# Attention with decay and a gated convolution layer: the last 64 tokens of two batches in one output chunk, three slots for gated products side by side, and another order of the work

## The chip, the cores and the metric

The kernel runs on one core of one Trainium2 chip. The metric is device time in microseconds (us) of one execution. Engines are named as the profile names them: PE is TensorE (PEld its weight loads), DVE VectorE, ACT ScalarE, POOL GpSimd, SP the engine that issues most DMAs (SPq its queue).

## What is computed

There are 8 batches of 8 heads, 576 tokens, 64 values per head. The first half is causal attention whose scores lose, from a key to a later query, the sum of the logs of a forget factor between them:

```python
scores = q @ k.T / sqrt(64) + (cum[query] - cum[key])   # cum = cumsum(log(f)), causal
attn   = softmax(scores);  x = attn @ v                  # x: [8, 576, 512], heads side by side
```

The second half is a layer on x with 512 inputs, 1024 inner channels and 512 outputs:

```python
h    = relu(x @ w_in)                                    # [8, 576, 1024]
conv = conv_w[0]*h[t-1] + conv_w[1]*h[t] + conv_w[2]*h[t+1]   # per channel, zero at both ends
out  = (h * sigmoid(conv)) @ w_out                       # [8, 576, 512], float32
```

## The kernel before

The program is a list of named tasks. Each task belongs to an engine, names the tasks it follows, and takes and gives slots of small pools (PSUM tiles `ps`, four of 128x1024; probability tiles, V tiles, inner tiles `ht` and `u`, gated products `hg`, output tiles `ob`). A long string, `ORDER` (line 18), gives the one order in which all tasks are issued, so it sets each engine's own order; `name@ENGINE` picks the engine where several can do a task. Each engine works through its tasks strictly in that order and waits where data or a slot is late.

The tasks, with their lines. A group `hb` of four heads is half a batch.

- `q`, `fi`, `rw`, `v`, `wi`, `wo` are loads on SP: transposing loads of q and k (L178), rows of the decay (L200, L201, L192, L194), V (L207), the weights (L496). `cl` (L170, L172, L184) clamps q and k rows on ACT or DVE; for the first two groups PE turns plain loads (`tp`, L164) and `cl` copies them out. `va` (L215, L217) casts V to 16 bits and `wic`, `woc` (L504) the weights, on POOL, ACT or DVE.
- `sd`, `so`, `st` are scores on PE (L310 and, for masks and the first heads' decay, L313 to L318); `ed`, `eo`, `et` their exponentials on ACT (L351, L368, L330); `md`, `mt` the causal masks of later groups on POOL (L354, L333).
- `pv` (L387, L392) is attention times V on PE, `n` (L400, L401) divides by the sum on DVE, `t` (L410) turns the result on PE and `tx` (L413) copies it to `xt`; the last two groups are turned by DMA (L416).
- For each batch `b` and each of 8 blocks of 128 inner channels: `f` (L425, PE) x times w_in, `r` (L435, ACT) relu, `c` and `d` (L440, L442, DVE) the two convolution steps, `a` (L445, ACT) tanh into `hg`, `g` (L449, DVE) the gated product in `hg`.
- `o` (L456, L460, PE) is the output: five chunks per batch, four of 128 tokens and one of the last 64; `e` (L466, L471) copies PSUM to `ob`, and `s` (L477, L482, L486) stores it.

In a chunk of 128 tokens the 8 gated blocks are 128x128 weights and 512 columns of w_out stream past them: 8 matmuls. In the chunk of 64 tokens (line 460) the weights are 64 columns wide; each block is used twice, with 256 columns of w_out each, the second into the other 64 partitions of PSUM: 16 matmuls, one copy of 128x256, two stores of 64x256. `hg` has two slots, one per batch in flight, given back when chunk 4 of the batch is done; the first plain loads of q and k also lie in them. In the last batch the output tasks are cut to one matmul each (`o7.c.ff`), so that they can start when one gated block is there, and each chunk has a copy and a store of its own.

Of the kernel before, what the change touches and what calls it, by code (L numbers as in the profile page):

```python
# [7 lines left out]
FP32 = mybir.dt.float32  # L8
FP16 = mybir.dt.float16
# [47 lines left out]
def kernel(  # L57
# [38 lines left out]
    dpool = ctx.enter_context(tc.tile_pool(name="dram", bufs=1, space=bass.MemoryType.DRAM))  # L96
# [49 lines left out]
    def ps_of(name):  # L146
        return ps_t[slot[name, "ps"]]


    def raw(hb):  # L150
        t = hg_t[slot[f"ld{hb}", "hg"]]
        return t.rearrange("p f s -> p (f s)").bitcast(FP32).rearrange("p (i x) -> p i x", i=4)
# [278 lines left out]
    def hg_of(b, ff):  # L431
        return hg_t[slot[f"h{b}", "hg"]][:, ff, :]
# [4 lines left out]
    def conv(b, ff, part):  # L437
        ht, u = ht_of(b, ff), u_t[slot[f"c{b}.{ff}", "u"]]
        if part == 0:
            nc.vector.scalar_tensor_tensor(u, ht[:, 0:S], cwt[:, ff, 0:1], ht[:, 1:1 + S], op0=ALU.mult, op1=ALU.add)  # L440
        else:
            nc.vector.scalar_tensor_tensor(u, ht[:, 2:2 + S], cwt[:, ff, 1:2], u, op0=ALU.mult, op1=ALU.add)  # L442

    def tanh(b, ff):
        nc.scalar.activation(hg_of(b, ff), u_t[slot[f"c{b}.{ff}", "u"]], AF.Tanh, scale=cw[:, ff, 1:2])  # L445

    def gate(b, ff):
        hv = hg_of(b, ff)
        nc.vector.scalar_tensor_tensor(hv, hv, 1.0, ht_of(b, ff)[:, 1:1 + S], op0=ALU.add, op1=ALU.mult)  # L449

    def ffn2(b, first, c, ffs):
        ps = ps_of(first)
        for ff in ffs:
            kw = dict(start=(ff == 0), stop=(ff == NFF - 1))
            if c < 4:
                nc.tensor.matmul(ps[:, 512 * (c % 2):512 * (c % 2 + 1)], hg_of(b, ff)[:, 128 * c:128 * (c + 1)],  # L456
                                 w_out_f16[:, ff, :], **kw)
            else:
                for a in range(2):
                    nc.tensor.matmul(ps[64 * a:64 * (a + 1), 0:256], hg_of(b, ff)[:, 512:576],  # L460
                                     w_out_f16[:, ff, 256 * a:256 * (a + 1)], skip_group_check=True, **kw)

    def evac(name, first, c, e):
        n = 1024 if c < 4 else 256
        ob = ob_t[slot[name, "ob"]].rearrange("p j c -> p (j c)")
        (nc.scalar.copy if e == "ACT" else nc.vector.tensor_copy)(ob[:, 0:n], ps_of(first)[:, 0:n])  # L466
# [206 lines left out]
```

## Time and profile before

| what | us |
|---|---|
| median of the three runs shown | 248.97 |
| these runs | 248.34, 248.97, 250.13 |
| span of the profiled execution, core 0 | 248.9 |
| PE, DVE, ACT, POOL busy in it | 232.9, 215.9, 211.1, 46.0 |
| mean granted TensorE clock | 0.998 |

The page gives the span as the profiled execution's time and no other time of that execution beside it. Busy time counts an instruction from its start to its end. Matmuls overlap, so their mean duration (379 ns for 512 columns) is more than the time from one to the next; the chain of waits, in which a group of eight takes 1.73 us, shows the latter. Times in windows and timelines are us from the span's start.

### The profile page before, as it was taken

How to read it: one execution, taken by the hardware profiler on the slowest of the kernel's cores; microseconds unless marked ns; L12 is line 12 of the kernel's file. 1: busy time of each engine (PE TensorE's matmuls, PEld its weight loads, DVE VectorE, ACT ScalarE, POOL GpSimd, SP SyncE). 2: the span in 40 equal slices, each digit the busy share in tenths (PEclk: the TensorE clock that was granted, in tenths of full speed). 3: DMA queues.
4: the chain of work that ended last, by engine and by line, in shares of the span. 5: the costliest groups of instructions: out<-in, count | busy, mean ns of one | idle time of the engine just before them, and what ended most of it. 6: DMA issues, size and time to landing. Idle time of an engine off the chain costs nothing.

```text
span 248.9 us, 6646 instructions
## 1 busy us (share of the span) xinstructions
PE 232.9 (94%) x2750; PEld 151.3 (61%) x2750; DVE 215.9 (87%) x328; ACT 211.1 (85%) x286; POOL 46.0 (18%) x76
## 2 busy tenths in 40 slices
PE   0899999879899999999999999999999999999993
PEld 0787785557556856666556765577557756645441
DVE  5654278999999999999999999997999999999961
ACT  2766958999999999979999899998999999767642
POOL 8000411101021501002203070045012502000000
PEclk9999999999999999999999999999999999999999
DMA  7987999999998999999999999899960590223345
GB/s 199 297 157 171 253 226 238 178 276 180 264 201 155 261 173 237 244 250 250 211 271 275 230 188 266 235 230 154 244 188 3 145 320 7 50 47 108 121 153 191
DMA packets 117062, 48.81 MB, mean 196 GB/s; under 512 B 106402, under 2 KB 107618, under 8 KB 117032
## 3 DMA queue, kind: packets, MB, share of 16 engines
q1 hardware_dynamic: 116578, 47.51, 85.3%
q0 software_dynamic: 208, 0.51, 0.7%
q8 instruction: 21, 0.34, 0.6%
q10 hardware_dynamic: 246, 0.37, 0.5%
q14 instruction: 9, 0.07, 0.1%
HBM read 21.11 MB, written 10.17 MB: 126 GB/s over the span
## 4 chain that ended last, share of the span: by engine, by line
PE 68%; DVE 12%; ACT 9%; DMA 6%; issue 3%; ACTq 0%; SPq 0%; DVEq 0%
PE ps L456 18%; PE ps L425 18%; PE ps L310 13%; PE ps L387 6%; PE ps L460 3%; DVE u L440 3%; DMA qk<-in_q_dram 3%; DVE u L442 3%; PE ps L318 2%; DMA u<-in_f_dram 2%; PE ps L410 2%; ACT pp L368 2%; PE ps L392 2%; ACT hg L445 2%; DVE hg L449 2%
## 5 line engine op out<-in xcount | busy, mean ns | idle before, releaser
L425 PE MATMUL ps<-xt,w_in_f 128*128 128x512 f16 (+1 forms) x512 | 68.4, 286 | 1.6 <-DMA xt<-xm 0.6
L368 ACT ACTIVATE pp<-ps 128x1024 f16<-128x1024 f32 x64 | 65.4, 1043 | 4.9 <-PE ps L310 2.6
L310 PE MATMUL ps<-qk 128*128 128x128 bf16 (+2 forms) x576 | 64.4, 241 | 1.8 <-DVE xm L401 0.6
L456 PE MATMUL ps<-w_out_f,hg 128*128 128x512 f16 x256 | 59.2, 379 | 0.0
L442 DVE SCALAR_TENSOR_TENSOR u<-ht,cwt,u 128x576 f32<-128x576 f16 x64 | 53.8, 854 | 1.4
L440 DVE SCALAR_TENSOR_TENSOR u<-ht,cwt 128x576 f32<-128x576 f16 x64 | 53.1, 837 | 2.3 <-ACT ht L435 2.2
L445 ACT ACTIVATE hg<-u,cw 128x576 f16<-128x576 f32 x64 | 48.9, 784 | 5.7 <-DVE u L442 5.7
L425 PEld LDWEIGHTS <-w_in_f 128*128 128x128 f16 x512 | 34.0, 98 | 31.0 <-issue 2.5
L310 PEld LDWEIGHTS <-qk 128*128 128x128 bf16 x576 | 39.6, 98 | 18.9 <-issue 3.8
L449 DVE SCALAR_TENSOR_TENSOR hg<-hg,ht 128x576 f16<-128x576 f16 x64 | 49.8, 800 | 1.0 <-ACT hg L445 0.9
L435 ACT ACTIVATE ht<-ps 128x576 f16<-128x576 f32 x64 | 41.3, 669 | 3.3 <-PE ps L425 3.2
L456 PEld LDWEIGHTS <-hg 128*128 128x128 f16 x256 | 24.0, 98 | 25.9 <-issue 0.2
L354 POOL TENSOR_SCALAR_AFFINE_SELECT pp<-pd 128x1024 f16<-128x1024 f32 x16 | 18.6, 1171 | 48.2 <-ACT pd L351 42.4
L387 PE MATMUL ps<-va,pp 128*128 128x65 f16 x640 | 24.6, 193 | 0.7 <-ACT pp L368 0.5
L401 DVE TENSOR_TENSOR xm<-ps,rc 128x896 f16<-128x896 f32 (+1 forms) x32 | 24.3, 758 | 1.1
L387 PEld LDWEIGHTS <-pp 128*128 128x128 f16 x640 | 22.4, 97 | 3.0 <-ACT pp L368 1.0
L351 ACT ACTIVATE pp<-ps 128x1024 f16<-128x1024 f32 x16 | 16.5, 1038 | 4.7 <-PE ps L315 2.4
L466 ACT COPY ob<-ps 128x1024 f32<-128x1024 f32 (+1 forms) x18 | 15.1, 838 | 3.4 <-PE ps L456 2.5
L351 ACT ACTIVATE pd<-ps 128x1024 f32<-128x1024 f32 x16 | 15.9, 1022 | 1.9 <-PE ps L310 1.9
L318 PE MATMUL ps<-mask,ident 128*128 128x512 bf16 (+1 forms) x40 | 14.8, 369 | 0.3 <-ACT xt L413 0.2
L184 DVE TENSOR_SCALAR qk<-qk,lim 128x2304 uint16<-128x2304 uint16 x12 | 11.2, 933 | 1.1 <-DMA qk<-in_k_dram 0.9
L333 POOL TENSOR_SCALAR_AFFINE_SELECT pt<-p 128x256 f16<-128x256 f32 x8 | 4.8, 596 | 38.6 <-ACT p L330 36.9
(86 smaller groups left out, 193.2 us busy)
## 6 DMA issues: line engine op xcount, KB each, us to landing
vf<-in_v_dram SPq DMA_DIRECT2D x32, 256.0 KB, 4.8
out_dram<-ob SPq DMA_DIRECT2D x14, 512.0 KB, 4.9
qk<-blank SPq DMA_DIRECT2D x8, 540.0 KB, 5.9
ob<-in_moe_w_in_dram SPq DMA_DIRECT2D x4, 512.0 KB, 4.8
ob<-in_moe_w_out_dram SPq DMA_DIRECT2D x4, 512.0 KB, 4.9
vf<-in_v_dram SPq DMA_DIRECT2D x8, 128.0 KB, 5.2
out_dram<-ob SPq DMA_DIRECT2D x4, 256.0 KB, 2.1
out_dram<-ob SPq DMA_DIRECT2D x15, 64.0 KB, 3.2
```

The source lines that it names most:

```text
L310: nc.tensor.matmul(o, tk[:, h * S + k0:h * S + k0 + 128], tq[:, h * S + q0:h * S + q0 + n], start=first, stop=last and not by_matmul(hb, h))
L351: nc.scalar.activation(o, ps_of(f"sd{i}").rearrange("p (s c) -> p s c", s=2), AF.Exp, scale=SCALE)
L368: nc.scalar.activation(pair(i)[:, s, 512:1536], ps_of(f"so{i}.{s}"), AF.Exp, scale=SCALE)
L387: nc.tensor.matmul(ps[:, c:c + D + 1], block(hb, h, m, n), va[:, h, m, 0:D + 1], start=(m == 0), stop=(m == n))
L401: nc.vector.tensor_tensor(xm[:, CUT * D * u:CUT * D * u + nj * k * D].rearrange("p (j x d) -> p j x d", x=k, d=D), got[:, :, :, 0:D], r.un ...
L425: nc.tensor.matmul(ps[:, t0:t1], w_in_f16[:, cc, 128 * ff:128 * (ff + 1)], xt[:, cc // 2, x:x + t1 - t0], start=(cc == 0), stop=(cc == NCC ...
L435: nc.scalar.activation(ht_of(b, ff)[:, 1:1 + S], ps_of(f"f{b}.{ff}")[:, 0:S], AF.Relu, scale=0.5)
L440: nc.vector.scalar_tensor_tensor(u, ht[:, 0:S], cwt[:, ff, 0:1], ht[:, 1:1 + S], op0=ALU.mult, op1=ALU.add)
L442: nc.vector.scalar_tensor_tensor(u, ht[:, 2:2 + S], cwt[:, ff, 1:2], u, op0=ALU.mult, op1=ALU.add)
L445: nc.scalar.activation(hg_of(b, ff), u_t[slot[f"c{b}.{ff}", "u"]], AF.Tanh, scale=cw[:, ff, 1:2])
L449: nc.vector.scalar_tensor_tensor(hv, hv, 1.0, ht_of(b, ff)[:, 1:1 + S], op0=ALU.add, op1=ALU.mult)
L456: nc.tensor.matmul(ps[:, 512 * (c % 2):512 * (c % 2 + 1)], hg_of(b, ff)[:, 128 * c:128 * (c + 1)], w_out_f16[:, ff, :], **kw)
```

## The change

The last 64 tokens of an even batch and the first 64 of the next, odd batch are neighbours in the output. The change lets them share one chunk of 128 tokens:

- The gated products lie in one tile `hg` of three slots side by side, 576 columns each, for every block of channels. The middle slot is for odd batches (pool `ho`), the outer two for even ones (pool `he`). The end of one batch and the start of its partner therefore touch, at columns 512 to 640 or at 1088 to 1216.
- In a pair whose even batch lies left, the even batch's four chunks begin at token 0 and the odd batch's at token 64; in the other pairs it is the other way round, and the shared chunk holds the odd batch's last 64 tokens and the even batch's first 64.
- Chunk 4 exists for odd batches alone. It follows the gated products of both batches, has 8 matmuls of 128x128 weights by 512 columns, one copy of 128x512, and one store of 128 rows (two of 64 rows where the tokens are not neighbours). Both `hg` slots come back after it.
- The order string is another one throughout. The four transposing-load groups, the weights and V stand in other places, some casts are on other engines, and the neighbours on each engine differ.

Beginning of the order string's line, before and after:

```diff
-dca cw ld0 ld0.0.0 tp0.0.0 dcl ld0.1.0 ld0.0.1 tp0.0.1 tp0.1.0 v0.0 ld1 ld0.1.1 ld1.0.1 ld1.0.0 dcs dck q2.1 ki@SP
...
+ld1 ld0 ld0.0.0 ld0.1.0 ld0.0.1 v0.0 ld0.1.1 ld1.0.1 ld1.0.0 cw dca dcl tp0.0.0 q2.1 tp0.0.1 cl0.0.0@ACT dcs
...
```

The rest, cut to its core:

```diff
-    RING, NP, NPT, NVA, NVF, NX, NRC, NXT, NHT, NU, NHG, NOB = 4, 6, 4, 4, 2, 2, 3, 2, 5, 4, 2, 3
+    RING, NP, NPT, NVA, NVF, NX, NRC, NXT, NHT, NU, NHG, NOB = 4, 6, 4, 4, 2, 2, 3, 2, 5, 4, 3, 3
...
-    hg_t = [cpool.tile([128, NFF, S], FP16, name=f"hg{t}") for t in range(NHG)]
+    hg_all = cpool.tile([128, NFF, NHG * S], FP16, name="hg")
...
-                 "hg": NHG, "ob": NOB, "pd": NPD, "p3": NP3})
+                 "he": 2, "ho": 1, "ob": NOB, "pd": NPD, "p3": NP3})
...
     def hg_of(b, ff):
-        return hg_t[slot[f"h{b}", "hg"]][:, ff, :]
+        t = 1 if b % 2 else 2 * slot[f"h{b}", "he"]
+        return hg_all[:, ff, S * t:S * (t + 1)]
...
+    def low(b):
+        return slot[f"h{b - b % 2}", "he"] == 0
+
+    def shift(b):
+        return 0 if low(b) == (b % 2 == 0) else S - 512
+
+    def shared(b, ff):
+        return hg_all[:, ff, 512:640] if low(b) else hg_all[:, ff, 2 * S - SL:2 * S + SL]
...
-            kw = dict(start=(ff == 0), stop=(ff == NFF - 1))
-            if c < 4:
-                nc.tensor.matmul(ps[:, 512 * (c % 2):512 * (c % 2 + 1)], hg_of(b, ff)[:, 128 * c:128 * (c + 1)],
-                                 w_out_f16[:, ff, :], **kw)
-            else:
-                for a in range(2):
-                    nc.tensor.matmul(ps[64 * a:64 * (a + 1), 0:256], hg_of(b, ff)[:, 512:576],
-                                     w_out_f16[:, ff, 256 * a:256 * (a + 1)], skip_group_check=True, **kw)
+            t = shift(b) + 128 * c
+            w = hg_of(b, ff)[:, t:t + 128] if c < 4 else shared(b, ff)
+            nc.tensor.matmul(ps[:, 512 * (c % 2):512 * (c % 2 + 1)], w, w_out_f16[:, ff, :], start=(ff == 0), stop=(ff == NFF - 1))
...
-        else:
-            for a in range(2):
-                e = nc.scalar if a and b == B - 1 else nc.sync
-                e.dma_start(outf[r:r + SL, 256 * a:256 * (a + 1)], ob[64 * a:64 * (a + 1), 0, 0:256])
+        elif shift(b):
+            nc.sync.dma_start(outf[b * S - SL:b * S + SL, :], ob[:, 0, :])
+        else:
+            nc.sync.dma_start(outf[b * S + 512:(b + 1) * S, :], ob[0:SL, 0, :])
+            nc.sync.dma_start(outf[(b - 1) * S:(b - 1) * S + SL, :], ob[SL:128, 0, :])
...
-            for c in range(5):
+            for c in range(4 + b % 2):
...
-                    behind=[f"o{b}.{c - 1}"] if c else [], give=[("hg", f"h{b}")] if c == 4 else [])
+                    behind=[f"o{b}.{c - 1}"] if c else [], give=[("he", f"h{b - 1}"), ("ho", f"h{b}")] if c == 4 else [])
```

Three places of the new order, engine by engine (line numbers of the changed program are one to seven higher). First SP, in the first 40 us, from a small load of V to the transposing loads of group 3 (`qk3`), before:

```order
L207 DMA vf0_89<-in_v_dram 64x8x64
L178 DMA_TRANSPOSE qk2_87<-in_q_dram 128x2304
L200 DMA qk1_86<-image_65 1x2304
L201 DMA qk1_86<-image_65 2x2304
L207 DMA vf0_89<-in_v_dram 128x8x64 x3
L200 DMA qk2_87<-image_65 1x2304
L201 DMA qk2_87<-image_65 2x2304
L496 DMA ob0_127<-in_moe_w_in_dram 128x2x512
L496 DMA ob1_128<-in_moe_w_in_dram 128x2x512
L178 DMA_TRANSPOSE qk3_88<-in_q_dram 128x2304
L496 DMA ob2_129<-in_moe_w_in_dram 128x2x512
L178 DMA_TRANSPOSE qk3_88<-in_k_dram 128x2304
```

and after:

```order
L208 DMA vf0_89<-in_v_dram 64x8x64
L179 DMA_TRANSPOSE qk2_87<-in_q_dram 128x2304
L503 DMA ob2_128<-in_moe_w_in_dram 128x2x512
L201 DMA qk1_86<-image_65 1x2304
L202 DMA qk1_86<-image_65 2x2304
L208 DMA vf0_89<-in_v_dram 128x8x64 x3
L503 DMA ob0_126<-in_moe_w_in_dram 128x2x512
L201 DMA qk2_87<-image_65 1x2304
L202 DMA qk2_87<-image_65 2x2304
L208 DMA vf1_90<-in_v_dram 128x8x64
L179 DMA_TRANSPOSE qk3_88<-in_k_dram 128x2304
L179 DMA_TRANSPOSE qk3_88<-in_q_dram 128x2304
```

Two loads of w_in stand just ahead of the first row shown here. So all four of them, and one of V's second tile, are now ahead of the transposing loads of group 3, three of them ahead of the row loads of group 1 (`qk1`).

Second ACT at the same time: the turned copies of groups 0 and 1 (`qk0`, `qk1`, written from PSUM) and the first exponentials (`pp`), before:

```order
L351 ACTIVATE pp0_95<-ps2_132 128x2x512
L170 ACTIVATE qk1_86<-ps3_133,lim_76 128x1152
L170 ACTIVATE qk1_86<-ps1_131,lim_76 128x1152
L368 ACTIVATE pp1_96<-ps0_130 128x1024
L368 ACTIVATE pp0_95<-ps1_131 128x1024
```

and after:

```order
L352 ACTIVATE pp0_95<-ps2_131 128x2x512
L171 ACTIVATE qk1_86<-ps3_132,lim_76 128x1152
L369 ACTIVATE pp0_95<-ps1_130 128x1024
L369 ACTIVATE pp0_95<-ps3_132 128x1024
L171 ACTIVATE qk1_86<-ps0_129,lim_76 128x1152
```

Two exponentials of the first heads moved ahead of ACT's second copy for group 1, on which the row loads of `qk1` wait.

Third DVE, among the convolution steps and gates of batch 0 up to the clamp of group 5 (`qk1`). A first step writes a `u` from an `ht`; the second step reads and writes the same `u`. Before, from the second block's second step, three instructions behind the first step of all:

```order
L442 SCALAR_TENSOR_TENSOR u1_122<-ht1_117,cwt_72,u1_122 128x576
L440 SCALAR_TENSOR_TENSOR u2_123<-ht2_118,cwt_72 128x576
L442 SCALAR_TENSOR_TENSOR u2_123<-ht2_118,cwt_72,u2_123 128x576
L449 SCALAR_TENSOR_TENSOR hg0_125<-hg0_125,ht0_116 128x576
L449 SCALAR_TENSOR_TENSOR hg0_125<-hg0_125,ht1_117 128x576
L215 CAST va3_94<-vf1_90 128x4x4x64
L440 SCALAR_TENSOR_TENSOR u3_124<-ht4_120,cwt_72 128x576
L440 SCALAR_TENSOR_TENSOR u0_121<-ht0_116,cwt_72 128x576
L440 SCALAR_TENSOR_TENSOR u1_122<-ht3_119,cwt_72 128x576
L442 SCALAR_TENSOR_TENSOR u1_122<-ht3_119,cwt_72,u1_122 128x576
L442 SCALAR_TENSOR_TENSOR u3_124<-ht4_120,cwt_72,u3_124 128x576
L184 TENSOR_SCALAR qk1_86<-qk1_86,lim_76 128x2304
```

and after, from the first step of all:

```order
L442 SCALAR_TENSOR_TENSOR u0_121<-ht0_116,cwt_72 128x576
L444 SCALAR_TENSOR_TENSOR u0_121<-ht0_116,cwt_72,u0_121 128x576
L442 SCALAR_TENSOR_TENSOR u1_122<-ht1_117,cwt_72 128x576
L444 SCALAR_TENSOR_TENSOR u1_122<-ht1_117,cwt_72,u1_122 128x576
L451 SCALAR_TENSOR_TENSOR hg_125<-hg_125,ht0_116 128x576
L442 SCALAR_TENSOR_TENSOR u2_123<-ht3_119,cwt_72 128x576
L451 SCALAR_TENSOR_TENSOR hg_125<-hg_125,ht1_117 128x576
L216 CAST va3_94<-vf1_90 128x4x4x64
L442 SCALAR_TENSOR_TENSOR u3_124<-ht4_120,cwt_72 128x576
L185 TENSOR_SCALAR qk1_86<-qk1_86,lim_76 128x2304
L444 SCALAR_TENSOR_TENSOR u3_124<-ht4_120,cwt_72,u3_124 128x576
L442 SCALAR_TENSOR_TENSOR u0_121<-ht2_118,cwt_72 128x576
```

The clamp of group 5 stands nine instructions behind the first convolution step, where it stood fourteen behind it, and from the third block on a second step no longer stands right behind its own first step.

On the other engines: POOL now casts 8 of V's 128x1024 tiles (4 before), 9 of the 64x256 (6), all four of w_in (3) and three of w_out (2); DVE 5 and 5 of V (9 and 4), ACT 3 and 2 (3 and 6). Over the whole program, the second convolution step stands right behind its own first step on DVE 17 times, 34 times before.

More of the change, by code (lines that the diff above doesn't have):

```diff
@@ L529 @@
             loads = [(p, 1, side) for p, side in parts] if hb == 0 else [(0, 2, side) for side in range(2)]
-            add(f"ld{hb}", "SP", [], lambda: None, take=["hg"])
+            add(f"ld{hb}", "SP", [], lambda: None, take=["he"])
             got = {}
@@ L537 @@
                 add(f"tp{hb}.{p}.{side}", "PE", [got[p, side]], lambda hb=hb, p=p, side=side: turn_qk(hb, p, side),
-                    take=["ps"], give=[("hg", f"ld{hb}")] if (p, side) == (1, 1) else [],
+                    take=["ps"], give=[("he", f"ld{hb}")] if (p, side) == (1, 1) else [],
                     behind=[f"tp{hb}.{x}.{y}" for x, y in parts] [:2 * p + side])
@@ L610 @@
             if ff == 0:
-                add(f"h{b}", "ACT", [f"d{b}.{ff}"], lambda: None, take=["hg"])
+                add(f"h{b}", "ACT", [f"d{b}.{ff}"], lambda: None, take=["ho" if b % 2 else "he"])
             add(f"a{b}.{ff}", "ACT", [f"d{b}.{ff}"], lambda b=b, ff=ff: tanh(b, ff), give=[("u", f"c{b}.{ff}")],
@@ L615 @@
         wo = [f"woc{j}" for j in range(4)]
+        before = [f"g{b - 1}.{ff}" for ff in range(NFF)]
         if last:
@@ L618 @@
                 for c in range(NKB):
-                    add(f"o{b}.{c}.{ff}", "PE", [f"g{b}.{ff}"] + (wo if ff == 0 else []),
+                    add(f"o{b}.{c}.{ff}", "PE", [f"g{b}.{ff}"] + (before if c == 4 and ff == 0 else []) + (wo if ff == 0 else []),
                         lambda b=b, c=c, ff=ff: ffn2(b, f"o{b}.{c & ~1}.0", c, [ff]),
@@ L623 @@
         else:
[L624 removed]
+            for c in range(4 + b % 2):
                 a = c // 2
                 first = f"o{b}.{2 * a}"
[L627 removed]
+                add(f"o{b}.{c}", "PE", [f"g{b}.{ff}" for ff in range(NFF)] + (before if c == 4 else []) + wo,
                     lambda b=b, c=c, first=first: ffn2(b, first, c, range(NFF)), take=["ps"] if c % 2 == 0 else [],
[L629 removed]
+                    behind=[f"o{b}.{c - 1}"] if c else [], give=[("he", f"h{b - 1}"), ("ho", f"h{b}")] if c == 4 else [])
         if last:
@@ L635 @@
             continue
-        for a in range(3):
+        for a in range(2 + b % 2):
             first, made = f"o{b}.{2 * a}", f"o{b}.{min(2 * a + 1, 4)}"
```

18 lines of the change are left out of this document (9 added, 9 removed).

## Prediction

> **What bounds the kernel now.** I read the page's top first, then stretches of the span with each engine's busy time, then the chain of waits, and last the groups of instructions and the timelines of the places that the change touches.
>
> ```profile
> span 248.9 us, 6646 instructions
> 0.00:40.20 40.20, 32.47 (x419) 26.01 (x420) 21.88 (x50) 25.08 (x27) 9.48 (x35) 1.00 0.96 220
> 40.20:82.20 42.00, 38.45 (x464) 24.44 (x461) 40.95 (x58) 41.61 (x58) 6.75 (x8) 1.00 1.06 210
> 82.20:201.20 119.00, 118.86 (x1478) 77.43 (x1478) 113.36 (x166) 111.89 (x154) 27.93 (x31) 1.00 0.97 216
> 220.40:240.70 20.30, 20.30 (x142) 10.14 (x142) 20.09 (x28) 14.15 (x22) 0.00 (x0) 1.00 0.31 107
> ```
>
> The columns behind the length are the busy us of PE, PEld, DVE, ACT and POOL, then the granted clock, the DMA engines' share and GB/s. From 82 us PE is never idle. Between 40 and 82 us DVE and ACT are full (40.95 and 41.61 of 42.00) and PE is not. In the first 40 us none of the three is full. The chain of waits says the same of the middle and the end:
>
> ```profile
> 96.24 0.99 PE ps L460 x16
> ...
> 100.41 1.96 PE ps L425 x16
> ...
> 103.36 0.44 PE ps L310 x4
> 103.80 1.73 PE ps L456 x8
> ...
> 217.44 2.89 DMA xt<-xm
> 220.38 2.61 PE ps L425 x20
> ...
> 243.90 1.01 PE ps L460 x16
> 244.94 0.37 ACT ob L471
> ```
>
> Here one task of PE follows the other without a gap, and each row gives a task's true time: an output chunk of 128 tokens 1.73, one of 64 tokens 0.99, a gate-input block 0.98 (two in 1.96), a head's off-diagonal scores 0.44. Adding such times in program order, I estimate 222.2 us of work on PE. Its last matmul ends at 244.9, so PE stood empty for 22.7 us, nearly all of it early:
>
> ```profile
> 71.45 1.89 PE L456 MATMUL ps<-w_out_f,hg 128*128 128x512 f16 x8
> ...
> 87.10 0.67 PE L410 MATMUL ps<-ident,xm 128*128 128x128 f16 x9
> ```
>
> At 87.60, when batch 1's last transposes (t5) are through, the tasks that stand before that point add up to 66.8, so 20.8 us are lost by then. From there to 244.9 are 157.3 us for 155.4 of work: 1.9 lost. So the time is PE's work, plus what PE loses while DVE and ACT feed the first two batches, plus 4 us of last copy and store. A saving on DVE or ACT counts only where it lets PE start earlier.
>
> **The change, term by term.** The sum is made against the profiled execution: span 248.9, which is the median of the runs shown (248.97) within 0.1, so nothing is added for what lies around it.
>
> ```profile
> L442 DVE SCALAR_TENSOR_TENSOR u<-ht,cwt,u 128x576 f32<-128x576 f16 x64 | 53.8, 854 | 1.4
> L184 DVE TENSOR_SCALAR qk<-qk,lim 128x2304 uint16<-128x2304 uint16 x12 | 11.2, 933 | 1.1 <-DMA qk<-in_k_dram 0.9
> L460 PE MATMUL ps<-w_out_f,hg 128*64 128x256 f16 x128 | 8.5, 275 | 0.0
> L413 DVE COPY xt<-ps 128x1152 f16<-128x1152 f16 x10 | 7.2, 751 | 1.0 <-PE ps L410 1.0
> L215 DVE CAST va<-vf 128x1024 f16<-128x1024 f32 x9 | 7.2, 797 | 5.2 <-DMA vf<-in_v_dram 5.2
> L215 POOL CAST va<-vf 128x1024 f16<-128x1024 f32 x4 | 4.6, 1161 | 33.5 <-DMA vf<-in_v_dram 33.5
> L217 DVE CAST va<-vf 64x256 f16<-64x256 f32 x4 | 2.0, 489 | 0.0
> L471 ACT COPY ob<-ps 128x512 f32<-128x512 f32 x3 | 1.8, 587 | 3.3 <-PE ps L456 3.3
> ```
>
> *1. Work on PE: -1.0.* Eight chunks of 16 half matmuls (L460, 0.99 each as the chain has them, since two halves run beside each other) become four chunks of eight full ones at the 1.73 of L456: 7.92 against 6.92. The output side of the full chunk is the form of L456, its weights are 128 columns that straddle two slots; I see no reason for another price. All of it lies where PE never waits, so it counts in full.
>
> *2. Copies and stores: nothing.* Eight copies of 128x256 (0.37 on ACT, the chain's last row) become four of 128x512 (0.59): 0.6 us less on ACT and DVE together, in stretches where PE has work in front of it. Fewer store issues on SP end behind the loads. The cover is PE's backlog; without it this would be a gain of 0.6 at most.
>
> *3. The slots: nothing.* Before, a batch's first tanh waits for the fourth chunk of the batch two earlier. For odd batches that holds still; even batches have two slots among them and wait less. What stands behind an odd batch's first tanh on ACT waits 0.74 longer for the fuller chunk at three places, with PE at work meanwhile.
>
> *4. The first 40 us: +1.2.* On ACT two exponentials now stand ahead of the last turned copy of heads 4 to 7, and on SP three loads of w_in and, before the transposes of the fourth group, one more of V.
>
> ```profile
> 15.26 3.44 SPq L178 DMA_TRANSPOSE qk<-in_q_dram  x1
> 19.90 0.32 SPq L200 DMA_DIRECT2D qk<-image  x1
> ...
> 31.14 4.66 SPq L178 DMA_TRANSPOSE qk<-in_k_dram  x1
> ...
> 39.39 0.88 DVE L184 TENSOR_SCALAR qk<-qk,lim 128x2304 uint16<-128x2304 uint16 x1 [0.90 <-DMA qk<-in_k_dram]
> 40.19 0.81 DVE L440 SCALAR_TENSOR_TENSOR u<-ht,cwt 128x576 f32<-128x576 f16 x1
> ```
>
> The row write (19.90) waits for that copy, which two exponentials push back to about 22.7; behind it on SP stand three V loads, a w_in load, another row write, a V load and then the two transposes, the second of which ended its issue at 35.8 and landed by 39.39. I put the end of that issue between 35.8 and 37.5, so the first convolution step (c0.0, 40.19) starts 0 to 1.7 later. The bytes give the other bound: 512 KB of w_in and 256 KB of V more ahead of it, at the 220 GB/s of the first 40 us, are 3.5 us, if no DMA engine was idle (0.96 busy). Below nothing: 0.3, if the exponentials done earlier free ACT sooner. I take 1.2, near SP's rows, since SP stood idle from 18.70 (15.26 and 3.44) to 19.90 and now stays so until 22.7, and some of the bytes move into that gap.
>
> *5. DVE up to batch 1's transposed input: +0.5.* Between c0.0 and that point DVE gains three copies of xt (0.75 each), a clamp (0.93) and a small cast (0.49), and loses a second convolution step (0.85) and two casts of V (0.80 each). A step that reads what the one before it wrote also costs more:
>
> ```profile
> 64.48 0.81 DVE L440 SCALAR_TENSOR_TENSOR u<-ht,cwt 128x576 f32<-128x576 f16 x1
> 65.33 0.82 DVE L442 SCALAR_TENSOR_TENSOR u<-ht,cwt,u 128x576 f32<-128x576 f16 x1
> ...
> 68.31 1.66 POOL L504 CAST w_out_f<-ob 128x1024 f16<-128x1024 f32 x1 [8.65 <-DMA ob<-in_moe_w_out_dram]
> 68.98 1.60 DVE L184 TENSOR_SCALAR qk<-qk,lim 128x2304 uint16<-128x2304 uint16 x1
> ...
> 75.00 0.87 DVE L184 TENSOR_SCALAR qk<-qk,lim 128x2304 uint16<-128x2304 uint16 x1
> 75.79 0.81 DVE L440 SCALAR_TENSOR_TENSOR u<-ht,cwt 128x576 f32<-128x576 f16 x1
> 76.52 0.75 DVE L449 SCALAR_TENSOR_TENSOR hg<-hg,ht 128x576 f16<-128x576 f16 x1
> ...
> 210.70 1.04 POOL L215 CAST va<-vf 128x1024 f16<-128x1024 f32 x1
> 211.77 0.92 DVE L440 SCALAR_TENSOR_TENSOR u<-ht,cwt 128x576 f32<-128x576 f16 x1
> ```
>
> From a first step to its own second step are 0.85 (64.48 to 65.33), to a gate 0.73 (75.79 to 76.52). There were 34 such neighbours, 8 of them in this stage; now there are 17, and 2: six times 0.12 is 0.7 less. In all 2.25 + 0.93 + 0.49 - 0.85 - 1.60 - 0.72 = +0.5.
>
> *6. Casts that go to POOL: +0.6.* In this stage POOL has one cast of 128x1024 more. Beside one such cast a clamp took 1.60 in place of 0.87 (+0.73); at the end of another, at 211.77, a first step took 0.92 in place of 0.81 (+0.11). I take 0.6, nearer the first, whose place in the program is nearer. The Trainium skill, "SBUF — State Buffer", section "Who interferes with whom", says that a DVE instruction with two SBUF inputs and a GpSimd instruction that reads SBUF exclude each other, the second blocked until the first is done. By that rule every such cast could cost DVE its whole 1.04. The trace agrees only in part: 0.73 and 0.11.
>
> DVE reached the end of this stage at 86.2 and PE the end of t5 at 87.6. With terms 4 to 6 DVE gets there at 86.2 + 2.3 = 88.5, with 66.9 of PE's work standing ahead of batch 2's first block (f2.0): 21.6 lost in place of 20.8, **+0.8**.
>
> *7. After that: -0.9.* PE lost 1.9 behind t5. By the same adding, up to the last attention product DVE now has 5 us less to do than then, ACT 2.5 less, PE 2.6 less, so PE should wait less. None of it back, or all, are the bounds; half is my choice.
>
> *8. The end: +0.2.*
>
> ```profile
> 245.34 0.49 SPq L486 DMA_DIRECT2D out_dram<-ob  x1
> out_dram<-ob SPq DMA_DIRECT2D x4, 256.0 KB, 2.1
> out_dram<-ob SPq DMA_DIRECT2D x15, 64.0 KB, 3.2
> ```
>
> The last copy is one of 512 columns, 0.59 in place of 0.37, and the last store one of 256 KB, which landed in 2.1, against 64 KB in 3.2 (and 3.5 for the last, 245.34 to the end). That is +0.2 with the store as it is, -1.1 if it lands as its form did.
>
> **Sum:** -1.0 + 0.8 - 0.9 + 0.2 = -0.9 from 248.9: **248.0 us**.
>
> **The rivals.** *A: PE is fed sooner.* The three loads of w_in fill SP's gap, c0.0 is not late (1.2 less than I took), and all 1.9 of the later losses go: 248.0 - 1.2 - 1.0 = 245.8. For it speaks that neighbours on DVE that wait for each other are halved; against it, that DVE's work in the early stage grows. *B: POOL holds DVE off.* The cast in the stage costs its full 1.04 (+0.4) and the later ones eat what term 7 gives (+0.9): 249.3, no change that can be told. This is the way it would go by the page named in term 6; the row at 211.77 speaks against it. *C: slower, by SP's queue.* The fourth group's transposes land 3.5 late as the bytes say (+2.3 over my term), and the next group's clamp, which by the same adding stands some 5 us nearer behind c0.0 on DVE than before, then waits for its own transposes, estimated at 1.5; term 7 falls away (+0.9): 248.0 + 4.7 = 252.7. It decides once DVE's waits for these loads reach 2.1 in all, at which the time is that of before; with term 7 gone 1.2 are enough. For it: DMA at 0.96 and 1.06 in the first two stretches. Against it: SP's idle time ahead of 19.90. That the chunk itself saves nothing would need a full chunk at 1.98; no row of L456 has that.
>
> **Chances.** About 1% is what a measurement of this kernel tells from no change: under 246.5 is faster, over 251.4 slower. Forecast 0.38 (its own range 246.4 to 249.6, of which 0.02 is faster), A 0.26 (0.25 faster), B 0.14, C 0.22 (0.18 slower). So faster 0.27, same 0.55, slower 0.18. The range, 244.8 to 251.9, reaches past A by the store's 1.1 less a little and into C, and leaves out some 0.2.
>
> **What would show it.** Of term 1, four groups of 1.73 for the shared chunks and no 128x256 form; of 4, c0.0 near 41.4 and DVE's clamp waiting for a DMA just before; of 5 and 6, f2.0 near 88.5 and the lengthened DVE rows beside POOL's casts; of 7, PE's idle time behind f2.0 under 1.5; of 8, 4 us from the last matmul to the end. I am wrong if PE is idle behind 90 us, or if c0.0 starts before 40 or after 43.

## The result, and the profile after

| kernel | median, us | runs | ratio to before on the same chip | 95% interval |
|---|---|---|---|---|
| before | 249.54 | 18 | | |
| after | 251.42 | 18 | 1.0068 | 1.0048 to 1.0089 |
| after, a second time on another chip (before 250.75 there) | 252.46 | 10 | 1.0062 | 1.0028 to 1.0096 |

The medians are over all runs; the ratios leave out runs that are over 1.5% longer than the fastest of their kernel (one of after's 18). The change costs 0.7%, 1.7 us. I forecast 0.9 us less. The time lies inside the range, the direction is wrong.

The page of the profiled execution of after begins so; its own time was 251.4, 1.8 more than its span.

```profile
span 249.6 us, 6448 instructions
PE 229.2 (92%) x2654; PEld 146.6 (59%) x2654; DVE 209.9 (84%) x324; ACT 207.6 (83%) x277; POOL 54.2 (22%) x85
```

The same stretches as for before, with the columns as there, and the last 9 us added:

```profile
0.00:40.20 40.20, 30.01 (x416) 24.17 (x417) 20.47 (x48) 25.60 (x27) 11.99 (x38) 1.00 1.04 227
40.20:82.20 42.00, 38.95 (x538) 26.47 (x537) 40.91 (x62) 40.72 (x56) 7.88 (x10) 1.00 1.05 216
82.20:201.20 119.00, 118.98 (x1383) 74.81 (x1383) 111.90 (x162) 111.42 (x153) 31.75 (x35) 1.00 1.00 209
220.40:240.70 20.30, 20.24 (x112) 9.43 (x110) 18.05 (x25) 13.57 (x22) 0.00 (x0) 1.00 0.33 111
240.70:249.60 8.90, 2.11 (x10) 0.78 (x8) 0.69 (x1) 1.65 (x3) 0.00 (x0) 0.86 0.44 162
```

Up to 240.7 nothing speaks for a slower kernel: from 82 on PE is as full as before, with less work on DVE. The last row does: in 8.9 us PE works 2.11. Before, it worked up to 4.0 from the end. The timeline of the end of after shows why (PE's last row starts at 230.99 and ends at 242.81):

```profile
230.99 11.82 PE L467 MATMUL ps<-w_out_f,hg 128*128 128x512 f16 x54
...
235.92 1.95 SPq L488 DMA_DIRECT2D out_dram<-ob  x3
...
239.66 0.59 ACT L477 COPY ob<-ps 128x512 f32<-128x512 f32 x1 [1.51 <-PE ps L467]
240.69 0.59 ACT L477 COPY ob<-ps 128x512 f32<-128x512 f32 x1 [0.45 <-PE ps L467]
241.30 4.90 SPq L483 DMA_DIRECT2D out_dram<-ob  x4
243.52 0.69 DVE L477 COPY ob<-ps 128x512 f32<-128x512 f32 x1 [4.47 <-PE ps L467]
244.29 1.07 ACT L477 COPY ob<-ps 128x512 f32<-128x512 f32 x2 [3.01 <-DVE ob L477]
```

The copy at 243.52 is e7.2. The bracket puts its wait down to PE, but PE had ended all its work at 242.81, so something else came last. The two copies behind it on ACT (e7.3 and e7.1) waited for it, and the last stores for them. The chain of waits of after points at the other thing, a store:

```profile
236.57 0.91 ACT ob L472
237.50 1.55 DMA out_dram<-ob
239.05 4.37 issue
243.52 0.70 DVE ob L477
244.29 0.59 ACT ob L477
244.88 0.49 ACTq L676
```

e7.2 writes an output buffer `ob`. There are three, and a task takes the one that came back first. Played through the order of after, this gives e7.2 the buffer of e6.1, which comes back with the store s6.1, the last of the three issues at 235.92; in the order of before it gives e7.2 the buffer of s5.1, a store whose issue had ended by 234.5, 6.9 ahead of the copy. s6.1 was issued at 237.50, behind two others of 512 KB: s6.0, and s3.1, the store of batch 3's second pair of chunks, whose copy had run at 169.8 and which the order of after issues 66 us behind that copy. The chain shows the store for 1.55 and then 4.37 of "issue", time for which it shows no cause; that the buffer came back only at about 243.4 is my reading, which the experiment "own slot" tests. The end of the span is 249.6 - 242.8 = 6.8 behind the last matmul, and 4.0 before: 2.8 lost, on top of a PE that was done 2.1 earlier in this execution (242.8 against 244.9). A run takes some 1.8 more than its span: the 248.9 of before's first profile is a run of about 250.7, slower than the median that I set it equal to.

### The profile page after: what moved, and what is told of

It reads as the page before. It is cut to its first block, busy times and chain, and to the rows that moved or that the text cites. A ratio compares the mean times of both kernels' runs of the same rounds, so it can differ in the third digit from the quotient of the medians.

```text
span 249.6 us, 6448 instructions
## 1 busy us (share of the span) xinstructions
PE 229.2 (92%) x2654; PEld 146.6 (59%) x2654; DVE 209.9 (84%) x324; ACT 207.6 (83%) x277; POOL 54.2 (22%) x85
## 4 chain that ended last, share of the span: by engine, by line
PE 59%; ACT 10%; DMA 9%; SPq 8%; DVE 6%; issue 4%; ACTq 0%; POOL 0%; DVEq 0%; POOLq 0%
PE ps L467 20%; PE ps L426 18%; PE ps L311 11%; PE ps L388 6%; SPq L179 5%; ACT pp L369 3%; PE ps L411 3%; ACT hg L447 3%; DMA qk<-in_k_dram 3%; DMA out_dram<-ob 2%; DMA u<-in_f_dram 2%; PE ps L393 2%; DMA vf<-in_v_dram 2%; DVE xm L402 2%; ACT ht L437 2%
## 5 line engine op out<-in xcount | busy, mean ns | idle before, releaser
L426 PE MATMUL ps<-xt,w_in_f 128*128 128x512 f16 (+1 forms) x512 | 70.9, 286 | 1.7 <-ACT ht L437 0.8
L467 PE MATMUL ps<-w_out_f,hg 128*128 128x512 f16 x288 | 66.6, 379 | 0.1
L311 PE MATMUL ps<-qk 128*128 128x128 bf16 (+2 forms) x576 | 63.6, 240 | 3.0 <-DMA qk<-image 1.7
L442 DVE SCALAR_TENSOR_TENSOR u<-ht,cwt 128x576 f32<-128x576 f16 x64 | 54.6, 861 | 3.0 <-ACT ht L437 3.0
L444 DVE SCALAR_TENSOR_TENSOR u<-ht,cwt,u 128x576 f32<-128x576 f16 x64 | 52.6, 840 | 1.2 <-POOL va L218 0.5
L426 PEld LDWEIGHTS <-w_in_f 128*128 128x128 f16 x512 | 34.7, 98 | 30.3 <-issue 2.0
L437 ACT ACTIVATE ht<-ps 128x576 f16<-128x576 f32 x64 | 42.3, 672 | 9.1 <-PE ps L426 5.3
L451 DVE SCALAR_TENSOR_TENSOR hg<-hg,ht 128x576 f16<-128x576 f16 x64 | 47.6, 770 | 1.6 <-ACT hg L447 1.6
L467 PEld LDWEIGHTS <-hg 128*128 128x128 f16 x288 | 27.1, 98 | 29.5 <-DVE hg L451 0.2
L401 DVE RECIPROCAL rc<-ps 128x14 f32<-128x14 f32 (+1 forms) x32 | 6.7, 208 | 10.7 <-ACT pp L369 7.3
```

The source lines that it names most:

```text
L311: nc.tensor.matmul(o, tk[:, h * S + k0:h * S + k0 + 128], tq[:, h * S + q0:h * S + q0 + n], start=first, stop=last and not by_matmul(hb, h))
L426: nc.tensor.matmul(ps[:, t0:t1], w_in_f16[:, cc, 128 * ff:128 * (ff + 1)], xt[:, cc // 2, x:x + t1 - t0], start=(cc == 0), stop=(cc == NCC ...
L437: nc.scalar.activation(ht_of(b, ff)[:, 1:1 + S], ps_of(f"f{b}.{ff}")[:, 0:S], AF.Relu, scale=0.5)
L467: nc.tensor.matmul(ps[:, 512 * (c % 2):512 * (c % 2 + 1)], w, w_out_f16[:, ff, :], start=(ff == 0), stop=(ff == NFF - 1))
```

## The experiments

All times beside the kernel before on the same chip, whose median was 250.6 to 250.8 in these runs.

**Before, once more.** No edit.

> The kernel before, unchanged, for a second profile of it: the profiled execution had a span of 248.9, while runs of after took 1.8 more than their span, so that the median of before, 249.5, speaks for a typical span near 247.8. If the first profile was a slow one, this one shows which waits of the first (0.6 of PE on the transposed input of batch 7, 3.5 between 40 and 82) are not there in every execution; expected 247.8, with the last matmul ending 4 before the end of the span as in the first.

One run, 250.34, span 248.6. So the first profile was no exception: this one is alike, except for 0.7 in the first 40 us (c0.0 at 39.45, against 40.19), and the expected 247.8 was wrong. PE's last row of the timeline:

```profile
243.55 1.06 PE L460 MATMUL ps<-w_out_f,hg 128*64 128x256 f16 x16
```

The last matmul ends at 244.6, again 4.0 ahead of the end.

**After, once more.** No edit.

> The kernel after, unchanged, beside the others on one chip: for a second profile of its end. Theory S: again the copy e7.2 waits 4 or more on DVE for s6.1, the end of the span is 6.5 to 7 behind the last matmul, the ratio is 1.005 to 1.009. If the end is 4 to 5 behind the last matmul this time, the wait is chance.

Ratio 1.0062. The end is again 6.8 behind the last matmul (251.9 and 245.13); the wait is no chance. The rows are from two windows of the timeline:

```profile
41.97 0.88 DVE L185 TENSOR_SCALAR qk<-qk,lim 128x2304 uint16<-128x2304 uint16 x1 [1.33 <-DMA qk<-in_q_dram]
42.77 0.81 DVE L442 SCALAR_TENSOR_TENSOR u<-ht,cwt 128x576 f32<-128x576 f16 x1
...
88.37 1.14 PE L426 MATMUL ps<-xt,w_in_f 128*128 128x512 f16 x8
...
233.31 11.82 PE L467 MATMUL ps<-w_out_f,hg 128*128 128x512 f16 x54
...
245.86 0.69 DVE L477 COPY ob<-ps 128x512 f32<-128x512 f32 x1 [4.50 <-PE ps L467]
```

This execution came 2.3 later from f2.0 on, and 2.0 later at the first convolution step. Of these 2.0, the longer wait for the transposing load made 0.9 (1.33 in place of 0.44); 1.1 were there before it, at the clamp ahead (39.77 against 38.63). They go at least in part with TensorE's clock. From 27 to 30 us it was granted at 0.50 here, and at 1.00 in the first profile of after; a mask matmul of 512 columns took 0.63 here and 0.38 there. PE was 0.4 late before this stretch and 1.1 late behind it. A window and a row of this execution (the clock is the third number from the end):

```profile
28.00:29.00 1.00, 1.00 (x9) 0.65 (x7) 0.00 (x0) 0.18 (x1) 0.00 (x0) 0.50 1.36 219
```

```profile
29.11 0.63 PE L319 MATMUL ps<-mask,ident 128*128 128x512 bf16 x1
```

Why the clock fell in this execution and not in the other is open, and so is how many of the other runs it fell in.

**Early store.** Only the late store's place in the order string changes.

```diff
-g7.5 s3.1 a7.7
+g7.5 a7.7
...
-pv13.0 s3.2
+pv13.0 s3.1 s3.2
```

> The kernel after, with one store moved: batch 3's second pair of chunks (s3.1) is issued right ahead of s3.2, some 8 us after its copy, instead of 66 us after it between s6.0 and s6.1. Theory S (a staging slot is held): in the kernel after, the copy e7.2 at 243.52 waited until the 512 KB store s6.1, issued at 237.50 behind two others of 512 KB, had landed and given its slot back, while the last matmul had ended near 242.8; with the slot given back early e7.2 runs at about 241, the last copy (e7.1) ends near 243.4 instead of 245.36, and the span shrinks from 249.6 to about 247.7: 251.4 becomes 249.5. Rival T (the transfers themselves): the end is set by how long the last stores' data take; one store of 512 KB less in the last 14 us gives a gain too, of the same size. Rival H (the head: convolutions and casts placed anew cost more than the end gives back): the time stays within 0.4 of 251.4.

250.25, ratio 0.9987 (0.9956 to 1.0017): 0.8% below after, the forecast of S and T. The timeline of its end:

```profile
230.25 11.82 PE L467 MATMUL ps<-w_out_f,hg 128*128 128x512 f16 x54
234.44 2.18 SPq L488 DMA_DIRECT2D out_dram<-ob  x2
...
240.61 3.65 SPq L483 DMA_DIRECT2D out_dram<-ob  x4
241.29 0.69 DVE L477 COPY ob<-ps 128x512 f32<-128x512 f32 x1 [3.61 <-DMA out_dram<-ob]
242.06 1.07 ACT L477 COPY ob<-ps 128x512 f32<-128x512 f32 x2 [1.48 <-DVE ob L477]
```

Here the bracket of e7.2 does name the store: played through, e7.2 still takes the buffer that s6.1 gives back. With one store of 512 KB ahead of it in place of two, s6.1 gave it back sooner. The copy runs 2.2 earlier than in after, and the end is 5.5 behind the last matmul (247.6 - 242.07), not yet 4.

**Own slot.** The late store stays; the last batch's third and fourth chunk get a buffer of their own.

```diff
-    ob_t = [cpool.tile([128, 2, D_MODEL], FP32, name=f"ob{t}") for t in range(NOB)]
+    ob_t = [cpool.tile([128, 2, D_MODEL], FP32, name=f"ob{t}") for t in range(NOB + 1)]
...
+    def room_of(b, c):
+        return ob_t[NOB] if c & ~1 == 2 else ob_t[slot[f"e{b}.{c & ~1}", "ob"]]
...
-                    take=["ob"] if c % 2 == 0 else [], behind=[f"e{b}.{c - 1}"] if c % 2 else [])
+                    take=["oz" if c == 2 else "ob"] if c % 2 == 0 else [], behind=[f"e{b}.{c - 1}"] if c % 2 else [])
```

> The kernel after, its order untouched, the late store s3.1 included; only the last batch's third and fourth chunks get a fourth output buffer of their own (the room comes from two 128x128 constants that now lie in the convolution's buffers). Theory S: e7.2 no longer waits for s6.1 and runs at about 241; the last copy ends near 243.4, the span is about 247.7, the time 249.5. Rival T: three stores of 512 KB still stand ahead of the last five, the last data land as late as before, and the time stays within 0.5 of 251.4. Rival H: within 0.4 of 251.4 as well, but with the last copy done 1.9 earlier it could not be told from T by the time alone; the row of the last copy tells.

250.07, ratio 0.9988 (0.9956 to 1.0021), though the three stores of 512 KB are issued as in after:

```profile
231.35 11.82 PE L466 MATMUL ps<-w_out_f,hg 128*128 128x512 f16 x54
236.27 1.95 SPq L490 DMA_DIRECT2D out_dram<-ob  x3
...
241.66 3.11 SPq L485 DMA_DIRECT2D out_dram<-ob  x4
242.13 0.69 DVE L479 COPY ob<-ps 128x512 f32<-128x512 f32 x1 [2.72 <-PE ps L466]
242.85 1.07 ACT L479 COPY ob<-ps 128x512 f32<-128x512 f32 x2 [1.22 <-DVE ob L479]
```

e7.2 now runs ahead of the last matmul's end (243.17), and the end is 4.9 behind that. T falls: the same stores are all still there, and what took the time was the wait of e7.2 for its buffer.

**Both ends.** The two edits together, and one more.

```diff
-s7.3 o7.1.6 s7.2
+s7.2 s7.3 o7.1.6
```

> The kernel after with the early store and the last batch's own output buffer together, and the last batch's stores s7.2 and s7.3 exchanged on SP's queue. In the kernel with the early store alone the copy e7.2 still waited 4.9 for a store, until 241.29, the last copies queued behind it, and the last store was issued at 243.93, 1.9 behind the last matmul (242.07); with the buffer alone it was 1.2. Theory S: nothing waits for a slot, the last store is issued 0.9 behind the last matmul, the end comes 4.2 to 4.4 behind that matmul, and the time is 1.0 below that of the early store alone: 249.2 on a chip where before takes 250.5, so it beats both. Rival T (the stores' data set the end): as with each alone, ratio 0.998 to 1.000.

250.15, ratio 0.9985 (0.9953 to 1.0017). The end is 4.5 behind the last matmul (249.1, 244.60), near what S said, but the time is that of each edit alone; the 1.0 more is not there, or is smaller than what these intervals (0.8 us either way) can show. In the profiled execution PE was done 2.5 later than with the early store, after a first convolution step 1.1 later (41.39 against 40.26) and a wait of 1.1 at 87.

**All ends.** Three more moves of stores.

```diff
-n15.1 s4.1
+n15.1 s4.0 s4.1
...
-f7.0 s4.0 f7.1
+f7.0 f7.1
...
-a7.0 s5.0 g7.0
+a7.0 g7.0
...
-s5.1 a7.1
+s5.1 s5.0 a7.1
...
-        nc.sync.dma_start(outf[r:r + 128, :], room_of(b, c)[:, c % 2, :])
+        (nc.scalar if c == 1 else nc.sync).dma_start(outf[r:r + 128, :], room_of(b, c)[:, c % 2, :])
```

> The kernel with both end edits, and three more moves of stores: s4.0 goes ahead of s4.1 and s5.0 behind s5.1, so that no store of 512 KB follows the transposing load of batch 7's input on SP's queue, and the last store but for the shared chunk, s7.1, is issued by ACT right behind its copy. In the kernel with the early store that load was under way 4.7 (212.56 to 217.30) against 2.9 in before, and PE waited 0.5 to 0.7 for it; the last store left 0.3 to 0.8 behind its copy. Theory S (what the stores hold up costs time): 0.5 + 0.3 to 0.4 less than both ends, 249.3 where before takes 250.6, ratio 0.993 to 0.996. Rival V (between executions the first 40 us vary by more than this): 250.1, ratio 0.998.

249.96, ratio 0.9961 (0.9932 to 0.9991): 0.4% faster than before and 1.0% faster than after, the only complete version whose interval lies below 1. It is the best of four that were tried, so part of this may be chance. The reason I gave for it failed all the same. From its chain and its timeline:

```profile
214.40 4.79 DMA xt<-xm
```

```profile
244.80 0.39 ACTq L485 DMA_DIRECT2D out_dram<-ob  x1
```

With no store right behind it the transposing load still was under way 4.79, so the stores do not explain why it is longer than the 2.89 of before; that stays open. The last store, issued by ACT, ended its issue at 245.19 and the span 3.5 later; in own slot SP's last ended at 244.77, 3.3 ahead of the end. The Trainium skill, "Trainium Kernel Development and Optimization", section "Key Constraints", says that DMAs of all queues share the same engines and that a second issuing engine saves only issue time; these two figures agree, as nothing was gained behind the issue (3.5 against 3.3).

**The chunk alone**, with the order of before.

```diff
-n8.1 o2.4 g3.7
+n8.1 g3.7
...
-v5.4 e2.2@ACT fi12 s2.2 sd22
+v5.4 fi12 sd22
```

These are batch 2's lines of it; the same goes for batches 0, 4 and 6.

> The shared chunk with the order of before: the code of after, its three slots and full-width chunk, and the order of before with only the even batches' own fifth chunks, copies and stores struck out (4 of each). Theory: the chunk is worth its 1.0 of PE less 0.2 at the end, so 249.5 becomes 248.7, and the new order costs what lies between that and 251.4 (2.7). Rival: the old order was tuned to the half chunks, and the odd batch's full chunk, which stands as long in one place as two did in two, leaves ACT and DVE waiting there; then it is 249.5 to 250.5 and the new order cost only 1 to 2.

255.86, ratio 1.0214 (1.0175 to 1.0252): 5.3 slower, past even the rival. So the chunk, which takes 1.1 off PE's work, is not worth 1.0 wherever it is put.

**Even struck.** Only the removal, in the order of before, whose string loses the same tasks as above.

```diff
-            for c in range(5):
+            for c in range(4 + b % 2):
...
-        for a in range(3):
+        for a in range(2 + b % 2):
```

> The kernel before with the even batches' fifth chunks, copies and stores struck out and nothing in their place: the last 64 tokens of four batches are not computed. PE has 4.0 less to do than before. The shared chunk in the old order (255.9 against 250.6) did just this and made the odd batches' chunk full width. Theory K (the struck chunk was cover: PE worked on it while DVE finished what the next steps wait for, and now comes too early and waits): no more than 1 of the 4.0 is gained, so 249.5 to 251.5, and PE idles 3 us more than before. Rival W (the loss comes from the full chunk alone, which stands where PE is the bound): the 4.0 are gained, 246.6.

251.27, ratio 1.0020 (0.9994 to 1.0046): of the 4.0 taken off PE nothing is gained. K holds. Windows of before, once more, and of even struck:

```profile
82.20:201.20 119.00, 118.86 (x1481) 77.43 (x1479) 113.27 (x164) 111.79 (x155) 27.94 (x30) 1.00 1.00 214
```

```profile
82.20:201.20 119.00, 116.87 (x1432) 75.25 (x1431) 112.59 (x162) 110.87 (x154) 28.80 (x32) 1.00 1.03 213
```

PE stands empty 2.1 where it was full. One of the places, batch 2's struck chunk, in before's second profile and then in even struck:

```profile
140.98 1.04 PE L460 MATMUL ps<-w_out_f,hg 128*64 128x256 f16 x16
...
142.39 1.42 DVE L449 SCALAR_TENSOR_TENSOR hg<-hg,ht 128x576 f16<-128x576 f16 x2
...
143.70 2.15 POOL L354 TENSOR_SCALAR_AFFINE_SELECT pp<-pd 128x1024 f16<-128x1024 f32 x2 [2.98 <-ACT pd L351]
143.73 1.41 DVE L413 COPY xt<-ps 128x1152 f16<-128x1152 f16 x2
```

```profile
142.36 2.31 DVE L449 SCALAR_TENSOR_TENSOR hg<-hg,ht 128x576 f16<-128x576 f16 x2
142.79 4.08 POOL L354 TENSOR_SCALAR_AFFINE_SELECT pp<-pd 128x1024 f16<-128x1024 f32 x3 [2.10 <-ACT pd L351]
...
144.60 1.41 DVE L413 COPY xt<-ps 128x1152 f16<-128x1152 f16 x2
...
145.40 1.27 PE L310 MATMUL ps<-qk 128*128 128x64 bf16 x12 [1.10 <-DVE xt L413]
```

The half chunk at 140.98 was cover. Without it PE makes the next scores sooner, POOL's masks of them start 0.9 sooner and fall beside DVE's two gates, these take 2.31 in place of 1.42, the copy of xt comes later, and PE waits 1.10 for the PSUM tile it frees. The Trainium skill, "SBUF — State Buffer", section "Who interferes with whom", has DVE instructions with two SBUF inputs and GpSimd's reads of SBUF exclude each other; the 0.89 fits that rule, since a gate reads two tiles of SBUF and a mask reads one.

**Odd full.** The other half of the chunk: full width in batches 1, 3 and 5, nothing removed.

```diff
-            if c < 4:
-                nc.tensor.matmul(ps[:, 512 * (c % 2):512 * (c % 2 + 1)], hg_of(b, ff)[:, 128 * c:128 * (c + 1)],
+            if c < 4 or b % 2:
+                t = min(128 * c, S - 128)
+                nc.tensor.matmul(ps[:, 512 * (c % 2):512 * (c % 2 + 1)], hg_of(b, ff)[:, t:t + 128],
```

> The kernel before, with the fifth chunk of batches 1, 3 and 5 made full width: 8 matmuls of 128x128 by 512 columns on the last 128 tokens, a copy of 128x512, one store of the last 64; batch 7 and the even batches stay. PE has 0.74 more to do three times, 2.2 in all. Theory K: PE is not the bound at all of these places, and the time grows by 1 to 2.2 at most: 251.6 to 252.8. Rival W: each place costs more than its work, since ACT and DVE wait behind it, and most of the 5.3 that the shared chunk cost in the old order appears here: 254 to 256.

253.11, ratio 1.0095 (1.0063 to 1.0128): 2.4 slower (1.6 to 3.2 by the interval) for 2.2 of work. So in this order work added to PE counts in full as far as can be told, and work taken away does not count. The two halves make 0.5 + 2.4. Where the other 2.4 of the chunk's 5.3 lie is shown only in part: odd full leaves the last batch as it was, and there, in the chunk alone, PE waited 2.10 for batch 7's input, where it waited 0.57 in before:

```profile
224.01 1.36 PE L426 MATMUL ps<-xt,w_in_f 128*128 128x512 f16 x9 [2.10 <-DMA xt<-xm]
```

**The order alone**, with the early store and the half chunks put back.

```diff
-e0.1@ACT g2.0
+e0.1@ACT o0.4 e0.2@ACT g2.0
...
```

This is batch 0's line of it, without its store; the same goes for batches 2, 4 and 6.

> The new order with the old half chunks: the code of before (three hg slots in place of two, so that the order fits), the order of after with the early store, and the even batches' half chunk, copy and stores put back, each right behind the copy ahead of it. Compared with the early store alone (250.25 where before takes 250.56) it has 1.0 more of PE's work, and PE is busy from 82 to the end there. Theory C (the chunk pays where the order covers for it): about 1.0 slower than the early store alone, 251.2. Rival N (the new order, not the chunk, makes the middle contiguous, and the chunk gives nothing): 250.2. Rival M: the half chunk put back in a place nobody chose delays others as it did the other way round, 252 to 255.

258.94, ratio 1.0311 (1.0273 to 1.0348): M, and past its 252 to 255. PE waits for ACT's copies among others (1.7 in two waits), so this tells that each order fits its own tasks, and not what the chunk is worth in the new one.

**Chunk dearer, chunk halved.** That question by another way: the early store with the shared chunk made longer or shorter in its place.

```diff
+            if c == 4 and ff % 2 == 0:
+                nc.tensor.matmul(ps[:, 512:1024], w, w_out_f16[:, ff, :], start=(ff == 0), stop=(ff == NFF - 2))
```

```diff
+            if c == 4 and ff % 2:
+                continue
...
```

> The kernel with the early store, its shared chunks made dearer: four more matmuls of 128x128 by 512 columns in each, into the unused half of their PSUM tile, 0.87 more in each of four, 3.5 in all. Theory C (in the new order PE is the bound from 82 to the end, and work on it counts in full): 250.25 becomes 253.7. Rival K (as in the old order, where 4 us less of PE's work gave nothing, DVE and ACT are as late as PE): 251 to 252.

> The kernel with the early store, its shared chunks made cheaper: every second block of channels is left out of them, so the sum over the inner channels is incomplete in those rows; 0.87 less of PE's work in each of four, 3.5 in all. Theory C (PE alone is the bound behind 82): 246.8. Rival K (DVE and ACT are close behind; what PE gains it waits for): no more than 1 of the 3.5, 249.3 to 250.3. Both can hold in part: the share of the 3.5 that is gained is what a saving on PE is worth in this order, and so what the 1.0 of the shared chunk is worth.

Dearer: 253.27, ratio 1.0074 (1.0047 to 1.0102), 2.2 above the early store for 3.5 of work. Halved: 249.50, ratio 0.9920 (0.9886 to 0.9953), 1.7 below it. Neither theory holds alone: PE's work counts here by about half to two thirds, with some 0.3 of uncertainty in these shares. The windows of the early store, and of halved:

```profile
82.20:201.20 119.00, 118.98 (x1393) 75.07 (x1392) 111.53 (x162) 111.44 (x153) 32.94 (x38) 1.00 1.01 215
```

```profile
82.20:201.20 119.00, 116.33 (x1350) 73.11 (x1348) 111.57 (x160) 110.06 (x151) 35.02 (x40) 1.00 1.03 214
```

PE is empty for 2.7 as soon as it has less to do. Its longer waits in that stretch are put down to ACT (0.7 twice), to a cast of V on POOL (1.0) and to DVE (0.2), so no single engine is the one close behind it.

## Why the prediction was wrong

**The end (term 8) failed.** "The last copy is one of 512 columns ... That is +0.2 with the store as it is", and "4 us from the last matmul to the end". It was 6.8 in both profiles of after. I priced the last copy and the last store, and did not ask which buffer the copies of the last batch take and whose store gives it back; under the slots (term 3) I looked at `hg` alone. What was needed stood in the order: e7.2 is the last task to take a buffer, the one that s6.1 gives back, and s3.1 had moved from batch 3 to just ahead of s6.1. Shown, with the number: the end cost 2.8 in place of 0.2, and each of two edits takes back 0.8%, the whole loss. Own slot spares e7.2 the wait with the late store still in place; early store makes it shorter.

That the time lay inside the range is luck: the range reached so far up for rival C, of which nothing is seen below. Neither sign of being wrong came: c0.0 lay between 40 and 43 in both profiles of after, and PE was idle for 0.4 behind f2.0. Both signs looked at the stretches ahead of the end.

**Up to the last matmul the forecast held, partly by offsetting errors.** It put PE's end at 248.0 - 4.2 = 243.8. The two profiles of after have 242.8 and 245.1, and with the four kernels of the same order but for stores (242.1, 243.2, 244.6, 244.0) the mean is 243.6, 1.1 below the 244.8 of before's two. Add the 2.8 of the end, and it is the measured 1.7. The offset, in the mean of the six: f2.0 came at 86.9, 1.6 earlier than forecast, and from there to the last matmul were 156.7, 1.4 more than the forecast's 155.3.

- *Term 1, -1.0:* PE's output matmuls took 59.2 and 8.5 before; now they are one form.

```profile
L456 PE MATMUL ps<-w_out_f,hg 128*128 128x512 f16 x256 | 59.2, 379 | 0.0
```

```profile
L467 PE MATMUL ps<-w_out_f,hg 128*128 128x512 f16 x288 | 66.6, 379 | 0.1
```

  67.7 became 66.6, 1.1 less, as the term has it. That it "counts in full" since PE never waits there was wrong: by the two trials with the chunk's length, PE's work counts for half to two thirds there, and in the order of before the same chunk cost 5.3. A PE without gaps shows that nothing is late for it now, and not by how little.
- *Term 4, +1.2:* c0.0 at 40.74 and 42.77 in the two profiles of after; with the other four, 41.2 in the mean, 1.4 above before's two. The size was right, the path was not. The rows of after:

```profile
39.94 0.88 DVE L185 TENSOR_SCALAR qk<-qk,lim 128x2304 uint16<-128x2304 uint16 x1 [0.44 <-DMA qk<-in_q_dram]
40.74 0.81 DVE L442 SCALAR_TENSOR_TENSOR u<-ht,cwt 128x576 f32<-128x576 f16 x1
...
86.07 1.14 PE L426 MATMUL ps<-xt,w_in_f 128*128 128x512 f16 x8
```

  The wait for the load just ahead of it is there, as said, but it is no longer than in before (0.44 and 1.33; before 0.90 and 1.26). What came later is the clamp ahead of that wait: 38.63 and 39.77, against 37.62 and 36.53. The row write was issued at 22.89, near the 22.7 of the forecast, but not for ACT's copy, which was done at 20.34: it stood behind a transposing load whose issue took 5.17 in place of 3.44. Then PE waited 1.7 for a row load in both profiles of after, and not at all in before's two; that this made DVE late is likely, and not tested. Of rival C nothing is seen: from the wait ahead of c0.0 up to 88, DVE waited 0.6 and 1.9 for the transposing loads, and 0.9 and 2.3 in before.
- *Terms 5 and 6 (+0.5, +0.6):* f2.0 was forecast at 88.5 and started at 86.07 and 88.37. Less the 66.9 of work ahead of it, 19.2 to 21.5 were lost, against 20.8 before and 21.6 forecast. From c0.0 to that point were 45.7 in the mean of the six, against 47.4 and 47.9 in before: 1.9 less, where terms 5 and 6 have 1.1 more. Why is not shown as a whole. Term 6 went the other way: the clamps between 40 and 88 took 872 ns in the mean, against 963 in before's second profile (groups of instructions in that window), although POOL does more. So rival B has nothing for it in the clamps. (The transposes that end at 87.60, which the prediction calls batch 1's and t5, are batch 2's, and the last of them is t4.)

```profile
L185 DVE TENSOR_SCALAR qk<-qk,lim 128x2304 uint16<-128x2304 uint16 x9 | 7.8, 872 | 0.6 <-DMA qk<-in_q_dram 0.4 <-DMA qk<-in_k_dram 0.2
```

```profile
L184 DVE TENSOR_SCALAR qk<-qk,lim 128x2304 uint16<-128x2304 uint16 x8 | 7.7, 963 | 1.0 <-DMA qk<-in_q_dram 1.0
```

- *Term 7, -0.9:* PE was idle for 0.42 of the 156.74 from f2.0 to its last matmul (86.07 to 242.81), under the 1.5 named. But those 156.74 are 2.4 more than the work that I had added up for them (154.3), in place of 1.0 more: that sum of unit prices was not good to 1 us, and the term hung on it. In before, too, PE was idle for only 0.74 of the 157.3 from 87.60 on, of which I called 1.9 lost. And the 22.7 for which I said that PE "stood empty" hold 12.0 of idle time (244.9 less the 232.9 of busy time); the rest is work that took longer than its unit price.
- *Terms 2 and 3:* nothing in the profiles speaks of a cost of the fuller copies, or of the `hg` slots.

## What to carry to other kernels

When an order is changed, follow each pool's buffers through it to the last task, the output buffers too: ask of each of the last copies which store gives it its buffer, and what stands ahead of that store in its queue. The cost appears at the copy, and can stand under another engine's name. A saving on an engine without gaps counts in full only if the next engines are well behind; a trial that makes the same work shorter and one that makes it longer tell that in two runs. And before a sum is made against a profiled span, set that span against the times of the runs.

## What had not been expected of the hardware

- From f2.0 to the last matmul the two executions of after took 156.74 and 156.76; all of their 2.3 of difference arose ahead of it and was passed on to the end in full. In one of the two the granted clock was 0.50 from 27 to 30 us, with PE at work; the mean clock of that execution (0.987, against 0.995) hardly shows it.
- A store of 512 KB (s6.1) gave its buffer back 5.9 behind its issue with two of the same size just ahead (237.50 to about 243.4), and 4.9 with one (236.24 to 241.1). The second is also the median of such stores on the page of before; the first is read from the wait of e7.2.
